# Casting v of batch 1 on GpSimd, asking for the second quarter of w_in between two casts, and one up step moved ahead of a down step

## The chip, the cores and the metric

The kernel runs on one core of a Trainium2 chip. Its engines work beside each other, each on its own queue and in the order of that queue: TensorE (matmuls and transposes into PSUM), VectorE and ScalarE (elementwise work, both may read PSUM), GpSimd (elementwise work on SBUF, and here the issue of the weights' DMAs), and SyncE (issues the other DMAs). The metric is the device time of one execution in microseconds (us); lower is better. An engine waits for another through semaphores.

## The reference

Two layers in a row. The first is causal attention with a sliding window of 128 and a linear bias per head, for 8 batches, 8 heads, 576 positions and 64 values per head. The second takes the 4608 tokens with their 8 x 64 = 512 attention outputs through a hidden layer of 2048:

```python
scores = scale * np.matmul(q, k.transpose(0, 1, 3, 2))
bias = slopes[:, None, None] * (-np.abs(rel).astype(np.float32))[None, :, :]
mask = (rel >= 0) & (rel < window)
scores = np.where(mask, scores + bias[None], -1000000000.0)
attn = softmax(scores)                       # written out in the reference
x = np.matmul(attn, v)                       # -> [B*S, H*D]
h = x @ w_in
g = h * np.clip(h + 3.0, 0.0, 6.0) / 6.0
out = g @ w_out
```

Inputs and output are float32 in DRAM.

## The kernel before

**Attention.** The unit of attention is a group g: two heads of one batch, four groups per batch, 32 in all. For each group the kernel computes transposed scores for the diagonal blocks (`scd`) and the blocks beside the diagonal (`sco`), exponentials on ScalarE (`pd`, `po`), and for some groups the mask by an affine select on GpSimd (L348 for `pd`, L358 for `po`). Groups 4 to 7 (batch 1) have their off-diagonal blocks masked through a table added on TensorE, so only their diagonal blocks are masked on GpSimd, by two selects per group. Then come the products with v, in which a column of ones beside v gives the sum of the exponentials; VectorE takes the reciprocal and scales (L406 and L407 in `attend`, L395 and L396 in `values`). `back` transposes the result into `xT`.

**v.** v of a batch comes by five DMAs (`load_tokens`, L112; 128 tokens each, the last 64) as float32 into one of four load buffers, and is cast to bf16 into `vbuf`. For batch 1 VectorE does this in five casts (`cast_v`, L177): pieces 0 to 3 after the off-diagonal exponentials of group 6, two ahead of each of two units of the hidden layer, and the last piece after that. For batches 2 to 7 GpSimd does it in three casts (`cast_tokens`, L183 twice and L186): two of 128 x 1024 values and one of 64 x 512.

**q and k** of batches 1 to 3 are loaded in double pieces (`load_double`, L98), cast on GpSimd (`prepare_double`, L223; for each of k and q two casts of 128 x 576), transposed on TensorE (`wide_double`, L248, or `double`, L236) and copied to `kTb` and `qTb`.

**Hidden layer.** The tokens are cut in nine tiles of 512. A tile has 16 ups and 16 downs. An up (`moe_up`) is four matmuls (L445) into `hps`, a ScalarE instruction (L464) and a VectorE product (L465) that writes one of 16 slices of `gbuf`. Up number ms needs columns ms x 128 of w_in, so ups 4 to 7 need its second quarter, 8 to 11 its third. A down (`moe_down`) is four matmuls (L477) and needs one of four quarters of w_out; four downs make a block of 128 output rows, after which the block is copied out (L492). The order of ups of one tile and downs of the tile before it is written out in `ORDER`, one string for each block; `fill(n)` takes the next n units from that list, at places written out in the attention code, so the order of all work on each engine is fixed.

**Weights.** w_in and w_out come in quarters by DMAs that GpSimd issues (L166, L171), with a cast to bf16 on the way. The first quarter of w_in is asked for among the casts of v of batch 0, the second after the four casts of the first double piece of batch 1 (`prepare_double(1, 0, ...)`), the third and fourth after the next four casts. The four quarters of w_out are asked for at the end of the loop over groups 4 to 6, after the casts of v. The buffer of w_out serves before that as the room for the exponentials of batch 0: slices 4 and 5 hold `pd` of group 1.

**Around it.** After the w_out issues GpSimd masks group 7, casts the double pieces of batch 2, and between them does a memset (L624) into a load buffer; v of batch 2 (SyncE) waits for that memset. The masks, casts and weight issues all stand in GpSimd's one queue in the order of the program.

Of the kernel before, what the change touches and what calls it, by code (L numbers as in the profile page):

```python
# [18 lines left out]
def kernel(  # L19
# [9 lines left out]
    nc = tc.nc  # L29
# [6 lines left out]
    NP = H // 2  # L36
# [18 lines left out]
    w_out_sb = perm.tile([128, n_ms, d_model], BF16)  # L55
# [94 lines left out]
    def warm_up(n):  # L150
        w = ps_av.tile([128, 128], FP32, tag="av", name="w")
        for _ in range(n):
            nc.tensor.matmul(w, lhsT=ident, rhs=ident, start=True, stop=True)
# [11 lines left out]
    def load_w_in(g):  # L165
        nc.gpsimd.dma_start(  # L166
            out=w_in_sb[:, :, ts(g, 512)],
            in_=moe_w_in[:, ts(g, 512)].rearrange("(k p) f -> p k f", p=128))

    def load_w_out(g):  # L170
        nc.gpsimd.dma_start(  # L171
            out=w_out_sb[:, ts(g, 4), :],
            in_=moe_w_out[ds(g * 512, 512), :].rearrange("(m p) d -> p m d", p=128))

    def cast_v(b, j, copy):
        n = min(128, S - j * 128)
        copy(out=vbuf[b % 2][:n, j, :, 0:D], in_=ld[b, "v"][:n, j, :, :])  # L177

    def cast_tokens(b, nm):
        s = ld[b, nm]  # L180
        if nm == "v":
            for lo in (0, 2):
                nc.gpsimd.tensor_copy(  # L183
                    out=vbuf[b % 2][:, lo:lo + 2, :, 0:D].rearrange("p j h d -> p (j h) d"),
                    in_=s[:, lo:lo + 2, :, :].rearrange("p j h d -> p (j h) d"))
            nc.gpsimd.tensor_copy(out=vbuf[b % 2][:LAST, 4, :, 0:D], in_=s[:LAST, 4, :, :])  # L186
            return
        for j in range(NQ):
            m = min(128, S - j * 128)
            nc.gpsimd.tensor_copy(out=tbuf[:m, :, j, :],  # L190
                                  in_=s[:m, j, :, :].rearrange("p (i e) d -> p i (e d)", e=2))
# [8 lines left out]
    def prepare(g, copies):  # L200
        for nm, copy in zip("qk", copies):
            pr = prs.tile([128, RT * D], BF16, tag=f"pr{nm}", name="pr",
                          padded_shape=[128, 2 * RT * D])
            copy(out=pr, in_=runs[nm][:, g % NP, :])
            st[g, nm] = pr
# [10 lines left out]
            copy(out=dst[:, hp, :, :].rearrange("p j c -> p (j c)")[:, 0:S].rearrange(  # L216
                "p (a t) -> p a t", t=RT), in_=tp.rearrange("p t a -> p a t"))

    def prepare_double(b, dp, copies, nms="kq"):
        for nm, copy in zip(nms, copies):  # L220
            pr = prs.tile([128, RT, 2 * D], BF16, tag=f"pr{nm}", name="pr2")
            for e in range(2):
                copy(out=pr[:, :, ts(e, D)],  # L223
                     in_=ldbuf["qk".index(nm)][:, ds((2 * dp + e) * RT * D, RT * D)].rearrange(
                         "p (t d) -> p t d", t=RT))
            st[b, dp, nm] = pr

    BANKS = {"h": ps_h, "av": ps_av, "o": ps_o}
# [31 lines left out]
    def tables_diag(g):  # L260
        scd = ps_sc.tile([128, 2, 512], FP32, tag="sc", name="scd")
        st[g, "scd"] = scd
        for e in range(2 if diag_tabled(g) else 0):
            t = tab[:, 2 * (g % NP) + e, 1:2, :]
            nc.tensor.matmul(scd[:, e, :].rearrange("p (j c) -> p j c", j=4), lhsT=ident,
                             rhs=t.to_broadcast([128, 4, 128]), start=True, stop=False)
# [26 lines left out]
    def tables_off(g):  # L293
        hp = g % NP
        sco = ps_sc.tile([128, 2, 512], FP32, tag="sc", name="sco")
        st[g, "sco"] = sco
        if full(g):
            for e in range(2):
                h = 2 * hp + e
                t = tab[:, h, 0:1, :]  # L300
                nc.tensor.matmul(sco[:, e, 128:512].rearrange("p (j c) -> p j c", j=3),
                                 lhsT=ident, rhs=t.to_broadcast([128, 3, 128]),
                                 start=True, stop=False)
                nc.tensor.matmul(sco[:, e, 0:128].rearrange("p (s c) -> p s c", s=2),
                                 lhsT=ident, rhs=tab[:, h, :, 0:64], start=False, stop=False)
# [26 lines left out]
    def exp_full(g):  # L332
        for e in range(2):
            exp_diag(g, e)
        exp_off_full(g)
# [113 lines left out]
    def up_begin(nt, ms, n):  # L449
        hps = ps_h.tile([128, NT], FP32, tag="h", name="hps")  # L450
        up_mms(nt, ms, 0, n, hps)
        begun[nt, ms] = hps, n
# [15 lines left out]
    def moe_down(nt, step):  # L468
# [10 lines left out]
        if part == 3:  # L479
# [11 lines left out]
            else:  # L491
                nc.vector.tensor_copy(out=osb, in_=ops[nt, sub])  # L492
                nc.sync.dma_start(out=out[rows, :], in_=osb)

    ORDER = [("UUDUDUDUD", "UUDUDUDUD", "UUDUDUDD", "UUDDDD"),
             ("DDDD", "UUDUDUDUD", "UUDUDUDUD", "UUDUDUDDUU"),
             ("DDDD",) * 4]
    units = [(0, moe_up, step) for step in range(16)]
    for nt in range(1, n_nt + 1):
        ups, downs = iter(range(16)), iter(range(16))  # L500
        for c in "".join(ORDER[0 if nt == 1 else 2 if nt == n_nt else 1]):
            units.append((nt, moe_up, next(ups)) if c == "U" else (nt, moe_down, next(downs)))
    at = [0]

    def fill(n):
        for _ in range(n):
            if at[0] == len(units):
                return
            nt, fn, step = units[at[0]]
            if fn is moe_up and done[0] < NP * (min((nt * NT + NT - 1) // S, B - 1) + 1):  # L510
                return
            fn(nt if fn is moe_up else nt - 1, step)
            at[0] += 1

    V, P, A = nc.vector.tensor_copy, nc.gpsimd.tensor_copy, nc.scalar.copy
# [24 lines left out]
    def first_batch():  # L540
        prepare(0, (V, A))
        warm_up(20)
        tables_diag(0)
        tables_off(0)
        warm_up(10)
        transposes(0, (V, A))
        scores_diag(0)
        prepare(1, (P, V))
        transposes(1, (V, V))
        scores_off(0)  # L550
        exp_full(0)
        scores_diag(1)
        prepare(2, (P, P))
        tables_off(1)
        transposes(2, (V, V))
        scores_off(1)
        exp_full(1)
        scores_diag(2)
        prepare(3, (P, V))
        tables_off(2)  # L560
        transposes(3, (V, V))
        scores_off(2)
        exp_full(2)
        scores_diag(3)
        scores_off(3)
        exp_full(3)
        cast_v(0, 0, V)
        cast_v(0, 1, P)
        load_w_in(0)
        cast_v(0, 2, V)  # L570
        cast_v(0, 3, V)
        cast_v(0, 4, P)
        for dp in range(2):
            for nm in "kq":
                load_double(1, dp, nm, nc.sync)
        load_tokens(1, "v")
        attend(0)
        attend(1)
        back(0)
        attend(2)  # L580
        back(1)
        prepare_double(1, 0, (P, P))
        load_w_in(1)
        attend(3)
        back(2)
        up_begin(0, 0, 3)
        back(3)
        wide_double(1, 0, "q", V)
        prepare_double(1, 1, (P, P))
        load_w_in(2)  # L590
        load_w_in(3)
        for dp in range(2):
            for nm in "kq":
                load_double(2, dp, nm, nc.sync)
        up_begin(0, 1, 3)
        done[0] = NP
        fill(1)
        wide_double(1, 0, "k", A)
        fill(2)

    def second_batch():
        for g in range(NP, 2 * NP - 1):
            if g < NP + 2:
                wide_double(1, 1, "kq"[g - NP], V)
            scores_diag(g)
            exp_diag(g, 0)
            exp_diag(g, 1)
            fill(1 if g == NP + 2 else 2)
            scores_off(g)
            exp_off_full(g)  # L610
            for n in range(2 if g == NP + 2 else 1):
                if g == NP + 2:
                    cast_v(1, 2 * n, V)
                    cast_v(1, 2 * n + 1, V)
                fill(1)
        cast_v(1, 4, V)
        for i in range(4):
            load_w_out(i)
        g = 2 * NP - 1
        scores(g)  # L620
        exp_diag(g, 0)
        exp_diag(g, 1)
        prepare_double(2, 0, (P, P))
        nc.gpsimd.memset(ldbuf[2][:, 0:1], 0.0)  # L624
        load_tokens(2, "v")
        prepare_double(2, 1, (P, P))
        for dp in range(2):
            load_double(3, dp, "k", nc.sync)
        load_tokens(3, "q")
        exp_off_full(g)  # L630
        fill(1)
        attend(NP)
        fill(1)
        attend(NP + 1)
        fill(1)
        back(NP)
        attend(NP + 2)
        fill(1)
        back(NP + 1)
        double(2, 0, "k", 0, "av", A)  # L640
        attend(NP + 3)
        back(NP + 2)
        double(2, 0, "k", 1, "av", A)
        wide_double(2, 0, "q", A)
        up_begin(1, 0, 3)
        back(2 * NP - 1)
        up_begin(1, 1, 3)
        done[0] = 2 * NP
        fill(2)
        scores_diag(2 * NP)  # L650
        scores_off(2 * NP)
# [98 lines left out]
```

## Time and profile before

| what | value |
|---|---|
| median of 3 runs | 335.48 us (335.27 to 336.54) |
| the profiled execution | 337.09 us, its span from first to last instruction 335.4 us |
| mean granted TensorE clock | 0.984 of full speed |
| TensorE matmuls busy | 314.2 us, 94% of the span |
| VectorE busy | 181.1 us, 54% |
| ScalarE busy | 198.5 us, 59% |
| GpSimd busy | 139.4 us, 42% |
| read from and written to DRAM | 36.70 MB and 9.44 MB |

Times in a timeline count from the start of the span. A row of it gives the start, the time until the end, the engine (PE is TensorE, DVE VectorE, ACT ScalarE, POOL GpSimd, SPq and POOLq the queues of SyncE and GpSimd), the line, the operation, what it writes and reads, and how many were merged; in brackets stands how long the engine was idle ahead of it, and what ended that. Shares are means over all stages: in the first 60 us the engines take turns at being late, and afterwards TensorE is busy nearly all of the time. The profile's busy time of a matmul is modelled, and neighbours overlap.

### The profile page before, as it was taken

Reading aid. Unit: us, or ns where it says so; the run is one execution under the profiler, and the core shown is the slowest. Engines: PE = TensorE matmul, PEld = TensorE weight load, DVE = VectorE, ACT = ScalarE, POOL = GpSimd, SP = SyncE. Lnnn points to the kernel's source line nnn. Section 1 sums busy time; section 2 is a strip of 40 time slices with the busy share of each in tenths; the row PEclk is TensorE's granted clock in tenths of the full one; section 3 lists DMA queues with packets and bytes.
Section 4 is the critical chain, followed back from the end, with each engine's and each line's share of the span. In section 5 each row is a group of like instructions: output and inputs, shape, how many; then the busy total and the mean of one; then the engine's idle time right before and its main releaser. Section 6 shows DMA issues by size and latency. Waiting matters only on the chain.

```text
span 335.4 us, 7019 instructions
## 1 busy us (share of the span) xinstructions
PE 314.2 (94%) x2707; PEld 169.2 (50%) x2747; DVE 181.1 (54%) x343; ACT 198.5 (59%) x339; POOL 139.4 (42%) x245
## 2 busy tenths in 40 slices
PE   7887938999999999999999999999999999999995
PEld 5463525544555455554577764454554444444442
DVE  6665597446434655466455554655556555445510
ACT  4746843677776775776577757675766344344401
POOL 8364390076459727573756375645333000000000
PEclk9998987999999999999999999999999999999999
DMA  7999999931999899989999997861021201000112
GB/s 286 203 336 223 323 159 221 245 99 50 211 199 221 182 201 226 227 160 220 222 164 171 209 226 162 172 153 53 33 71 44 71 29 37 31 31 33 62 53 73
DMA packets 128065, 51.08 MB, mean 152 GB/s; under 512 B 115616, under 2 KB 119968, under 8 KB 128032
## 3 DMA queue, kind: packets, MB, share of 16 engines
q1 hardware_dynamic: 122800, 44.61, 60.4%
q0 software_dynamic: 4224, 4.19, 8.0%
q10 hardware_dynamic: 1008, 1.84, 1.5%
q8 instruction: 21, 0.34, 0.5%
q14 instruction: 12, 0.10, 0.1%
HBM read 36.70 MB, written 9.44 MB: 138 GB/s over the span
## 4 chain that ended last, share of the span: by engine, by line
PE 80%; ACT 5%; DMA 4%; DVE 4%; POOL 3%; issue 2%; SPq 0%; POOLq 0%; DVEq 0%
PE ops L477 35%; PE hps L445 34%; PE scd L290 2%; DMA ldbuf<-in_q_dram 2%; DMA w_in_sb<-in_moe_w_in_dram 2%; PE av L385 2%; DVE vbuf L177 2%; PE av L377 2%; PE sco L322 2%; ACT r L464 1%; ACT xT L432 1%; DVE gbuf L465 1%; PE tb L426 1%; ACT kTb L238 1%; POOL pr L223 1%
## 5 line engine op out<-in xcount | busy, mean ns | idle before, releaser
L465 DVE SCALAR_TENSOR_TENSOR gbuf<-r,hps 128x512 bf16<-128x512 f32 x144 | 98.7, 686 | 108.2 <-ACT r L464 107.8
L464 ACT ACTIVATE r<-hps,bias 128x512 f32<-128x512 f32 x144 | 99.1, 690 | 91.3 <-PE hps L445 90.9
L445 PE MATMUL hps<-xT,w_in_sb 128*128 128x512 bf16 (+1 forms) x618 | 147.0, 362 | 4.9 <-DMA w_in_sb<-in_moe_w_in_dram 2.3
L477 PE MATMUL ops<-w_out_sb,gbuf 128*128 128x512 bf16 x558 | 139.2, 379 | 1.6 <-issue 1.1
L445 PEld LDWEIGHTS <-w_in_sb 128*128 128x128 bf16 x640 | 59.4, 99 | 57.8 <-issue 3.4
L477 PEld LDWEIGHTS <-gbuf 128*128 128x128 bf16 x576 | 53.6, 98 | 57.9
L348 POOL TENSOR_SCALAR_AFFINE_SELECT pd<-pd 128x512 bf16<-128x512 bf16 x48 | 30.1, 636 | 70.2 <-ACT pd L345 70.2
L358 POOL TENSOR_SCALAR_AFFINE_SELECT po<-po 128x512 bf16<-128x512 bf16 x48 | 30.5, 636 | 27.6 <-ACT po L355 26.8
L345 ACT ACTIVATE pd<-scd,bias_d 128x512 bf16<-128x512 f32 x48 | 32.1, 687 | 2.6 <-POOL vbuf L183 2.6
L355 ACT ACTIVATE po<-sco,bias_o 128x512 bf16<-128x512 f32 x48 | 33.3, 694 | 0.0
L492 DVE COPY osb<-ops 128x512 f32<-128x512 f32 x33 | 22.7, 688 | 18.7 <-PE ops L477 18.1
L190 POOL CAST tbuf<-ldbuf 128x512 bf16<-128x512 f32 (+1 forms) x45 | 25.5, 614 | 1.6 <-DMA qTb<-tbuf 1.6
L396 DVE TENSOR_TENSOR avs<-av,rc 128x384 bf16<-128x384 f32 (+1 forms) x48 | 23.5, 490 | 1.6
L385 PEld LDWEIGHTS <-pd 128*128 128x128 bf16 x192 | 14.3, 97 | 8.2 <-issue 0.5
L432 ACT COPY xT<-tb 128x576 bf16<-128x576 bf16 x13 | 8.3, 639 | 16.7 <-PE tb L426 16.7
L377 PE MATMUL av<-vbuf,po 128*128 128x65 bf16 x192 | 18.0, 193 | 0.0
L385 PE MATMUL av<-vbuf,pd 128*128 128x65 bf16 x192 | 17.3, 194 | 0.3 <-ACT kTb L238 0.2
L377 PEld LDWEIGHTS <-po 128*128 128x128 bf16 x192 | 14.3, 98 | 3.0 <-DVE avs L396 0.5
L361 ACT ACTIVATE p4buf<-sco,bias_d 128x64 bf16<-128x64 f32 x48 | 15.8, 329 | 0.0
L290 PEld LDWEIGHTS <-kTb 64*128 64x128 bf16 x256 | 7.2, 94 | 14.5 <-issue 10.8
L290 PE MATMUL scd<-qTb,kTb 64*128 64x128 bf16 x256 | 12.7, 219 | 1.8 <-DVE kTb L216 1.1
L223 POOL CAST pr<-ldbuf 128x576 bf16<-128x576 f32 x20 | 12.7, 664 | 3.9 <-DMA ldbuf<-in_k_dram 3.6
(93 smaller groups left out, 231.4 us busy)
## 6 DMA issues: line engine op xcount, KB each, us to landing
out_dram<-osb SPq DMA_DIRECT2D x33, 256.0 KB, 2.2
ldbuf<-in_v_dram SPq DMA_DIRECT2D x32, 256.0 KB, 5.3
ldbuf<-in_q_dram SPq DMA_DIRECT2D x20, 256.0 KB, 4.7
ldbuf<-in_k_dram SPq DMA_DIRECT2D x16, 256.0 KB, 4.7
ldbuf<-in_q_dram SPq DMA_DIRECT2D x12, 288.0 KB, 7.2
ldbuf<-in_k_dram SPq DMA_DIRECT2D x12, 288.0 KB, 7.6
w_in_sb<-in_moe_w_in_dram POOLq DMA_DIRECT2D x4, 512.0 KB, 8.3
w_out_sb<-in_moe_w_out_dram POOLq DMA_DIRECT2D x4, 512.0 KB, 9.2
```

The costliest lines, as they stand in the source:

```text
L190: nc.gpsimd.tensor_copy(out=tbuf[:m, :, j, :], in_=s[:m, j, :, :].rearrange("p (i e) d -> p i (e d)", e=2))
L290: nc.tensor.matmul(scd[:, e, ts(j, 128)], lhsT=kT[r, j, :], rhs=qT[r, j, :], start=first, stop=first or j == 3)
L345: nc.scalar.activation(out=pd[:, e, :, :].rearrange("p j c -> p (j c)"), in_=sc[:, e, :], func=ACT.Exp, bias=bias_d[:, h:h + 1], scale=scale)
L348: nc.gpsimd.affine_select(out=pd[:, e, :, :], in_=pd[:, e, :, :], pattern=[[0, 4], [1, 128]], channel_multiplier=-1, base=0, compare_op=AL ...
L355: nc.scalar.activation(out=po[:, e, :, :].rearrange("p j c -> p (j c)"), in_=sc[:, e, :], func=ACT.Exp, bias=bias_o[:, h:h + 1], scale=scale)
L358: nc.gpsimd.affine_select(out=po[:, e, :, :], in_=po[:, e, :, :], pattern=[[0, 4], [-1, 128]], channel_multiplier=1, base=-1, compare_op=A ...
L377: nc.tensor.matmul(out_av, lhsT=po[:, e, qt % 4, :], rhs=vb[:, qt - 1, h, :], start=True, stop=False)
L385: nc.tensor.matmul(out_av, lhsT=d, rhs=vb[:, qt, h, :], start=(qt == 0), stop=True)
L445: nc.tensor.matmul(hps[:, lo:hi], lhsT=w_in_sb[:, ks, ts(ms, 128)], rhs=xT[:, ks, ds(src, hi - lo)], start=(ks == 0), stop=(ks == n_ks - 1))
L464: nc.scalar.activation(out=r6, in_=hps, func=ACT.Relu, bias=bias3[:, 0:1], scale=1.0 / 6.0)
L465: nc.vector.scalar_tensor_tensor(out=gts[nt][:, ms, :], in0=r6, scalar=1.0, in1=hps, op0=ALU.min, op1=ALU.mult)
L477: nc.tensor.matmul(ops[nt, sub], lhsT=gts[nt][:, ms, ts(sub, 128)], rhs=w_out_sb[:, ms, :], start=(ms == 0), stop=(ms == n_ms - 1))
```

## The change

Three edits. First, v of batch 1 is cast by GpSimd in three casts (`cast_tokens(1, "v")`) after the two units that follow group 5's exponentials, in place of VectorE's five casts after those of group 6; the number of units that `fill` takes in each round stays. Second, the second quarter of w_in is asked for after the first of the four casts of `prepare_double(1, 0, ...)`; a one-column memset into slice 4 of the w_out buffer is put ahead of it. Third, in the order of tile 1's ups and tile 0's downs the first block has six ups in place of five, the additional one ahead of the last but one down, and the third block has three in place of four.

```diff
+    def second_w_in():
+        nc.gpsimd.memset(w_out_sb[:, 4, 0:1], 0.0)
+        load_w_in(1)
+
...
-    def prepare_double(b, dp, copies, nms="kq"):
+    def prepare_double(b, dp, copies, nms="kq", early=None):
         for nm, copy in zip(nms, copies):
             pr = prs.tile([128, RT, 2 * D], BF16, tag=f"pr{nm}", name="pr2")
             for e in range(2):
                 copy(out=pr[:, :, ts(e, D)],
                      in_=ldbuf["qk".index(nm)][:, ds((2 * dp + e) * RT * D, RT * D)].rearrange(
                          "p (t d) -> p t d", t=RT))
+                if early and (nm, e) == (nms[0], 0):
+                    early()
             st[b, dp, nm] = pr
...
-    ORDER = [("UUDUDUDUD", "UUDUDUDUD", "UUDUDUDD", "UUDDDD"),
+    ORDER = [("UUDUDUUDUD", "UUDUDUDUD", "UDUDUDD", "UUDDDD"),
...
-        prepare_double(1, 0, (P, P))
-        load_w_in(1)
+        prepare_double(1, 0, (P, P), early=second_w_in)
...
             scores_off(g)
             exp_off_full(g)
-            for n in range(2 if g == NP + 2 else 1):
-                if g == NP + 2:
-                    cast_v(1, 2 * n, V)
-                    cast_v(1, 2 * n + 1, V)
-                fill(1)
-        cast_v(1, 4, V)
+            fill(2 if g == NP + 2 else 1)
+            if g == NP + 1:
+                cast_tokens(1, "v")
         for i in range(4):
             load_w_out(i)
```

## The prediction

> **What bounds the kernel now.** I read the page first, then the time by stretches, then who waited for whom on TensorE, then each engine's timeline around the two waits found. The page's span, and stretches of the first 55 us (busy time of TensorE, its weight loads, VectorE, ScalarE and GpSimd, granted clock, DMA share, GB/s):
>
> ```profile
> span 335.4 us, 7019 instructions
> ```
> ```profile
> 30.00:35.00 5.00, 4.97 (x39) 2.76 (x39) 1.06 (x2) 2.40 (x3) 0.00 (x0) 0.66 1.24 205
> ...
> 40.00:45.00 5.00, 4.95 (x60) 2.62 (x59) 3.83 (x9) 5.00 (x9) 4.89 (x7) 1.00 0.88 198
> 45.00:50.00 5.00, 0.26 (x9) 0.17 (x6) 5.00 (x1) 1.01 (x2) 5.00 (x10) 0.84 1.14 182
> 50.00:55.00 5.00, 4.00 (x28) 2.16 (x28) 3.67 (x7) 0.69 (x1) 0.67 (x2) 0.50 1.22 200
> ```
>
> From some 60 us on the page's slices show TensorE at nine tenths or more, so whatever reaches TensorE earlier by then should reach the end earlier. Before that there are holes: from 45 to 50 there are 0.26 us of matmuls, and behind that the clock is 0.50; from 30 to 35 it is 0.66. TensorE's own waits, longest in total first, name what ended the two largest:
>
> ```profile
> PE wide L385 <- DVE vbuf L177: 5.7, 1, 5.7
> PE hps L445 <- DMA w_in_sb<-in_moe_w_in_dram: 2.3, 1, 2.3
> ```
>
> The first is the attention of group 4, waiting for the last cast of v. The group of v casts (shortest, median, longest in ns, first and last start), then GpSimd's timeline from that last start on:
>
> ```profile
> L177 DVE CAST vbuf<-ldbuf x8: 409/428/6218, 15.1 to 44.7; 128x512 bf16<-128x512 f32 x7, 64x512 bf16<-64x512 f32 x1
> ```
> ```profile
> 43.62 0.90 POOL L171 DMA_DIRECT2D w_out_sb<-in_moe_w_out_dram  x1
> 44.53 1.23 POOL L348 TENSOR_SCALAR_AFFINE_SELECT gbuf<-gbuf 128x512 bf16<-128x512 bf16 x2
> 45.70 2.49 POOL L223 CAST pr<-ldbuf 128x576 bf16<-128x576 f32 x4
> 48.14 0.09 POOL L624 MEMSET ldbuf<- 128x1 f32 x1
> 48.18 2.49 POOL L223 CAST pr<-ldbuf 128x576 bf16<-128x576 f32 x4
> ```
>
> A v cast takes 0.43 us at the median; the last, of half the size, takes 6.22. It starts at 44.7 while GpSimd works and ends at 50.9, just after GpSimd's unbroken row (44.53 to 50.67). I read it as shut out by GpSimd until that engine paused. TensorE's 5.7 us all come from this one instruction.
>
> The Trainium skill (SBUF — State Buffer, Who interferes with whom) says that a VectorE cast in a two-port mode and a GpSimd instruction exclude each other, and that the later one blocks until the first finishes. Taken literally the block would end with the first mask, at about 45.1; the trace has ten further GpSimd instructions pass first. Either a queue of them keeps the port, or the cast waited for something else: the second is rival E.
>
> **Part 1: v cast by GpSimd.** Five casts leave VectorE; three come to GpSimd, between the masks of groups 5 and 6. The same three for batch 2, with what follows, and a VectorE instruction beside them:
>
> ```profile
> 71.22 2.02 POOL L183 CAST vbuf<-ldbuf 128x1024 bf16<-128x1024 f32 x2
> 73.19 0.61 POOL L186 CAST vbuf<-ldbuf 64x512 bf16<-64x512 f32 x1
> 73.75 1.27 POOL L223 CAST pr<-ldbuf 128x576 bf16<-128x576 f32 x2
> ```
> ```profile
> 72.37 0.69 DVE L465 SCALAR_TENSOR_TENSOR gbuf<-r,hps 128x512 bf16<-128x512 f32 x1 [0.32 <-ACT r L464]
> ```
>
> Price on GpSimd: 2.02 + 0.61 = 2.6 us. The hole that takes it, ahead of group 6's masks; then the queues and the DMA issues between 27 and 28 us (KB each, us to landing):
>
> ```profile
> 40.10 1.23 POOL L348 TENSOR_SCALAR_AFFINE_SELECT gbuf<-gbuf 128x512 bf16<-128x512 bf16 x2 [2.92 <-ACT gbuf L345]
> ```
> ```profile
> q0 software_dynamic: 177, 0.17, 104.2%
> q1 hardware_dynamic: 149, 0.04, 17.5%
> issues: line engine op xcount, KB each, median us to landing
> w_in_sb<-in_moe_w_in_dram POOLq DMA_DIRECT2D x1, 512.0 KB, 11.1
> ldbuf<-in_v_dram SPq DMA_DIRECT2D x1, 128.0 KB, 12.1
> ```
>
> GpSimd is idle for 2.9 us, from 37.2 to 40.1, and 2.6 fit. But the last piece of v (128 KB) was issued before 27 and takes 12.1: it lands by 39, its cast ends by some 39.5. That is a **new wait** in GpSimd's queue. Behind it stand the masks of group 6, the four w_out issues, the masks of group 7, the casts of batch 2, and the memset that lets SyncE ask for v of batch 2. As part 2 brings TensorE and ScalarE earlier, group 6's masks will wait for the cast, no longer for their exponentials, and everything behind comes forward by only 0.6 us.
>
> What is late next? VectorE. Its next product needs the first row's result, and each attention group needs the pair of the second fence; the last of four such pairs is the third row:
>
> ```profile
> 45.30 0.71 ACT L464 ACTIVATE r<-hps,bias 128x512 f32<-128x512 f32 x1
> ```
> ```profile
> 51.47 0.20 DVE L406 RECIPROCAL rcw<-wide 128x10 f32<-128x10 f32 x1
> 51.70 0.82 DVE L407 TENSOR_TENSOR avs<-wide,rcw 128x640 bf16<-128x640 f32 x1
> ```
> ```profile
> 58.87 0.82 DVE L407 TENSOR_TENSOR avs<-wide,rcw 128x640 bf16<-128x640 f32 x1
> ```
>
> A pair takes 1.05 from 51.47 to 52.52, a product about 0.6 (0.69 less the overlap of neighbours); four of each make 6.6 us. Begun at 46.0 they end at 52.6; now they end at 59.7. **Gain 7.1 us.** The ends: 5.7 if the wait alone goes; 7.7 if the slow clock goes as well (4.00 us busy at 0.50, half of them lost) and TensorE alone sets the pace. I take 7.1, by VectorE's rows, the engine that is full there.
>
> The Trainium skill (Perfetto Trace Analysis, Optimizing Scalar/DVE Operations) warns that shifting work between these two engines may not help, since they share a port. The row at 72.37 speaks against it here: 0.69 us, the usual 686 ns of its group, while GpSimd casts v. The case is rival D.
>
> **Part 2: the second quarter of w_in asked for earlier.** GpSimd's order, the quarter's transfer in the chain that ended last, TensorE's next transposes, and the DMA rate at that time:
>
> ```profile
> 17.22 0.67 POOL L223 CAST pr<-ldbuf 128x576 bf16<-128x576 f32 x1 [0.88 <-DMA ldbuf<-in_k_dram]
> 20.60 2.11 POOL L223 CAST pr<-ldbuf 128x576 bf16<-128x576 f32 x3 [2.72 <-DMA ldbuf<-in_k_dram]
> ```
> ```profile
> 22.65 7.33 DMA w_in_sb<-in_moe_w_in_dram
> ```
> ```profile
> 22.77 0.68 PE L248 MATMUL tp<-ident,pr 128*128 128x128 bf16 x9
> ```
> ```profile
> 20.00:21.00 1.00, 0.83 (x23) 0.80 (x21) 0.91 (x2) 0.64 (x1) 0.40 (x1) 1.00 1.04 408
> ```
>
> The memset (the one at 48.14 took 0.09) waits for group 1's attention matmuls, which TensorE's timeline ends near 18.4. GpSimd idles for 2.72 us just there, so memset and issue (at most 0.90, as for w_out) cost its queue nothing. The transfer starts near 18.4 in place of 22.65 and lands between 25.7 (7.3, as now) and 29.5 (11.1, the slowest row above): TensorE no longer waits for it. Removed: 2.3 us, and the clock of 0.66 behind it (4.97 us with a third lost, 1.7), together 4.0. More it cannot be, for ScalarE is full from 40 to 45 (5.00 of 5).
>
> What it moves: the quarter is 1 MB as read, 0.5 as written, and now goes among the pieces of k and q while the engines carry 408 GB/s. It can take 0 to 2.6 us from them. The q cast ends at 22.7 and its transposes start at 22.77, so all of that reaches TensorE. I take the middle, 1.3. The third quarter's issue stands behind later q casts and slides the same way; for a wait there I take 0.4 (0 to 0.8). **Gain 4.0 - 1.3 - 0.4 = 2.3 us**, ends 0.6 and 4.0, and 0 if q is held for as long as w_in was.
>
> **Part 3: one up step earlier.** The same matmuls in another order. Two ups now follow each other within the first block; the later needs the PSUM bank that this copy frees, and the block's last down, which comes one step later, needs w_out's last quarter (issues from 44.0 to 44.4 us):
>
> ```profile
> 65.96 0.72 DVE L238 COPY kTb<-tp 128x512 bf16<-128x512 bf16 x1
> ```
> ```profile
> 68.65 1.03 PE L477 MATMUL ops<-w_out_sb,gbuf 128*128 128x512 bf16 x4
> ```
> ```profile
> w_out_sb<-in_moe_w_out_dram POOLq DMA_DIRECT2D x1, 512.0 KB, 12.9
> ```
>
> The copy ends at 66.7, and the up would begin at about 66.9. The quarter, issued at 43.62, lands at 56.5; the down, 9.4 earlier, would come at 59.3 even in its old place. So 0, ends plus and minus 1.0, one such group's length.
>
> **Sum:** 7.1 + 2.3 + 0 = 9.4 us. The profiled execution took 337.09, its span 335.4 (1.7 around it): 326.0 of span, 327.7 with the rest. The median of the runs is 335.48, 1.6 under the profiled one, so the forecast is **326.1**. What could cap it is k of batch 3 (issues from 59.0 to 59.5 us):
>
> ```profile
> ldbuf<-in_k_dram SPq DMA_DIRECT2D x1, 288.0 KB, 5.7
> ```
>
> Issued before 59, it lands by 64.7, or 64.1 with the memset 0.6 earlier; its cast at 73.75 wants it at 64.35. Gains beyond some 9.6 are partly given back there.
>
> **Rivals.** (B) Asking for w_in earlier only exchanges waits, q being held for as long as TensorE waited: part 1 alone, 328.4. For it: from 27 to 28 w_in's queue had 104% of the time against 17.5% for v's. Against: q's pieces are not v's. (C) q is hardly held and TensorE sets the pace: 7.7 + 4.0, less half of what is beyond 9.6, makes 10.7: 324.8. (D) The change does not do what it says, because a full GpSimd queue shuts out any VectorE instruction: the product due at 46.0 stands until 50.7 in the cast's place and all is as before, 335.5. Against: the row at 72.37. (E) The 6.22 us were a wait for v itself, landing at 50.3. Then its cast holds GpSimd until 50.9, and the megabyte put ahead makes that up to 53.5. Masks, w_out issues, masks and two casts (1.2 + 3.6 + 1.2 + 1.3) end at 60.8. TensorE wants those casts here:
>
> ```profile
> 57.37 0.44 PE L236 MATMUL tp<-ident,pr 128*128 128x128 bf16 x5
> ```
>
> That is 3.4 late: 338.9, slower; it turns slower once v lands after 49.5. Against: the landing by 39. The skill's literal lock rule leaves room for E; the cast's end beside the end of GpSimd's row does not.
>
> **Chances.** Forecast 0.50 (324.9 to 327.5), B 0.25, C 0.18, D 0.04, E 0.03. The range 323.7 to 329.5 takes in the forecast, B and C with the ends of part 3, and leaves out D and E. Faster by over 0.5% (1.7 us, about what a measurement of this kernel can tell from no change) 0.93, the same 0.04, slower 0.03.
>
> **What would show it.** Right: no VectorE instruction above 1.4 us and no wait of TensorE for vbuf; GpSimd's last v cast ending near 39.5; no clock of 0.5 at 50 us; the wait for w_in gone, with a shorter one for the q cast near 23; the transposes of 57.37 near 48. Wrong: a wait for w_in as long as before, or for its third quarter (B); a product of 5 us beside GpSimd's casts (D); GpSimd idle ahead of v's cast until past 49 (E); TensorE waiting for w_out, v of batch 2 or k of batch 3, where part of the gain would end.

## The result, and the profile after

Median 326.53 us (325.98 to 326.96, 4 runs) against 335.38 for the kernel before (334.7 to 336.54, 4 runs of it). The ratio is 0.9732, with a 95% interval of 0.9701 to 0.9763: 9.0 us faster, between 8.0 and 10.0. The forecast was 326.1.

The page's head after the change, and the stretches that had the holes:

```profile
span 324.2 us, 7015 instructions
## 1 busy us (share of the span) xinstructions
PE 311.6 (96%) x2707; PEld 168.5 (52%) x2747; DVE 173.9 (54%) x338; ACT 198.0 (61%) x339; POOL 141.2 (44%) x249
```
```profile
30.00:35.00 5.00, 4.84 (x55) 2.82 (x56) 4.30 (x7) 4.76 (x8) 2.13 (x4) 1.00 1.22 198
...
45.00:50.00 5.00, 4.50 (x74) 3.54 (x74) 4.36 (x9) 4.23 (x8) 4.22 (x8) 1.00 1.19 190
50.00:55.00 5.00, 5.00 (x48) 2.66 (x47) 2.05 (x4) 3.02 (x5) 0.00 (x0) 1.00 1.22 203
```

From 45 to 50 us TensorE is busy for 4.50 of 5 us where it had 0.26, and the granted clock is 1.00 in all three. TensorE's two longest waits are now small ones from the start and from the downs:

```profile
PE w L153 <- POOL ident masks.py:199: 1.4, 1, 1.4
PE ops L483 <- issue: 1.1, 7, 0.2
```

GpSimd's timeline around the new casts (L187 and L190 are the casts of v, L354 the masks, L171 the issues for w_out, L227 the casts of batch 2, L626 the memset that releases v of batch 2):

```profile
34.12 1.04 POOL L187 CAST vbuf<-ldbuf 128x1024 bf16<-128x1024 f32 x1
37.40 1.04 POOL L187 CAST vbuf<-ldbuf 128x1024 bf16<-128x1024 f32 x1 [2.24 <-DMA ldbuf<-in_v_dram]
38.38 0.61 POOL L190 CAST vbuf<-ldbuf 64x512 bf16<-64x512 f32 x1
38.95 1.21 POOL L354 TENSOR_SCALAR_AFFINE_SELECT gbuf<-gbuf 128x512 bf16<-128x512 bf16 x2
40.12 2.99 POOL L171 DMA_DIRECT2D w_out_sb<-in_moe_w_out_dram  x4
43.08 1.26 POOL L354 TENSOR_SCALAR_AFFINE_SELECT gbuf<-gbuf 128x512 bf16<-128x512 bf16 x2
44.26 2.50 POOL L227 CAST pr<-ldbuf 128x576 bf16<-128x576 f32 x4
46.69 0.11 POOL L626 MEMSET ldbuf<- 128x1 f32 x1
46.73 2.48 POOL L227 CAST pr<-ldbuf 128x576 bf16<-128x576 f32 x4
```

The wait in GpSimd's queue is there: 2.24 us for v to land. The last v cast ends at 38.99. Group 6's masks follow with no pause, so they wait for the cast and no longer for ScalarE. Counted with the w_out issues, GpSimd's unbroken row runs from 37.40 to 49.21. The part behind the issues, which held VectorE's cast in the kernel before (44.53 to 50.67), is as long as it was, 6.1 us from 43.08 to 49.21, and it now hurts nobody. The issues themselves held no cast: in the kernel before, four of VectorE's v casts ran beside them (41.27 to 44.52) in 0.41 to 0.57 us each. VectorE's fourth attention pair ends at 49.45 in place of 59.69, although it works beside that row:

```profile
48.63 0.82 DVE L413 TENSOR_TENSOR avs<-wide,rcw 128x640 bf16<-128x640 f32 x1
```

The second quarter of w_in, on GpSimd (L176 is the new memset), then its DMA row (KB, us to landing), then the transposes of q that the forecast expected to be held up:

```profile
19.06 0.10 POOL L176 MEMSET w_out_sb<- 128x1 bf16 x1 [1.50 <-PE wide L391]
19.10 0.74 POOL L166 DMA_DIRECT2D w_in_sb<-in_moe_w_in_dram  x1
20.80 2.02 POOL L227 CAST pr<-ldbuf 128x576 bf16<-128x576 f32 x3 [0.95 <-DMA ldbuf<-in_k_dram]
```
```profile
w_in_sb<-in_moe_w_in_dram POOLq DMA_DIRECT2D x1, 512.0 KB, 9.1
```
```profile
23.79 0.67 PE L254 MATMUL tp<-ident,pr 128*128 128x128 bf16 x9
```

Issued at 19.10, the quarter lands at 28.2. It takes 9.1 us in place of 7.3 but starts 3.6 earlier. In this execution TensorE waits no longer for it. The q cast ends at 22.82, as before the change (22.71), and the transposes start without a wait. They start a microsecond later than before because attention in this execution began as much later, ahead of anything that was changed: its first product with v comes at 17.89, against 16.77 in the profile of before. Executions differ by that much here; a second profile of the kernel before (before_again, below) has 17.77.

### The profile page after: what moved, and what is told of

Its sections match the earlier page's. It is cut to its first block, busy times and chain, and to the rows that moved or that the text cites. A ratio compares the mean times of both kernels' runs of the same rounds, so it can differ in the third digit from the quotient of the medians.

```text
span 324.2 us, 7015 instructions
## 1 busy us (share of the span) xinstructions
PE 311.6 (96%) x2707; PEld 168.5 (52%) x2747; DVE 173.9 (54%) x338; ACT 198.0 (61%) x339; POOL 141.2 (44%) x249
## 4 chain that ended last, share of the span: by engine, by line
PE 88%; ACT 5%; DVE 4%; issue 2%; POOL 0%; POOLq 0%
PE ops L483 38%; PE hps L451 36%; PE scd L296 3%; PE av L391 2%; ACT xT L438 2%; PE av L383 2%; PE sco L328 2%; ACT r L470 2%; PE tb L432 1%; PE w L153 1%; ACT kTb L244 1%; DVE qTb L220 1%; PE sco L307 1%; DVE kTb L220 1%; PE tp L254 1%
## 5 line engine op out<-in xcount | busy, mean ns | idle before, releaser
L451 PE MATMUL hps<-xT,w_in_sb 128*128 128x512 bf16 (+1 forms) x619 | 144.1, 357 | 2.3 <-ACT xT L438 0.6
L354 POOL TENSOR_SCALAR_AFFINE_SELECT pd<-pd 128x512 bf16<-128x512 bf16 x48 | 30.0, 633 | 61.1 <-ACT pd L351 61.1
L187 POOL CAST vbuf<-ldbuf 128x1024 bf16<-128x1024 f32 x14 | 14.2, 1040 | 2.2 <-DMA ldbuf<-in_v_dram 2.2
```

Of the source, the lines that this page charges most:

```text
L354: nc.gpsimd.affine_select(out=pd[:, e, :, :], in_=pd[:, e, :, :], pattern=[[0, 4], [1, 128]], channel_multiplier=-1, base=0, compare_op=AL ...
L451: nc.tensor.matmul(hps[:, lo:hi], lhsT=w_in_sb[:, ks, ts(ms, 128)], rhs=xT[:, ks, ds(src, hi - lo)], start=(ks == 0), stop=(ks == n_ks - 1))
```

## The experiments

Ten runs beside the two kernels. The medians of the kernel before lay between 335.8 and 336.1 us in these sessions, so gains are read from ratios; 0.01 of ratio is 3.36 us.

| run | median us | ratio to before, 95% interval |
|---|---|---|
| p1_only | 328.37 | 0.9769 (0.9736 to 0.9801) |
| p2_only | 334.39 | 0.9941 (0.9915 to 0.9967) |
| p3_only | 334.95 | 0.9971 (0.995 to 0.9993) |
| p1_p2 | 326.67 | 0.9718 (0.9687 to 0.975) |
| v4_act | 329.56 | 0.9812 (0.9763 to 0.9861) |
| pause | 329.56 | 0.9811 (0.9768 to 0.9854) |
| long_row | 338.21 | 1.008 (1.0053 to 1.0106) |
| v_dve_early | 327.5 | 0.9762 (0.9715 to 0.981) |
| w_in_ahead | 326.9 | 0.9728 (0.9691 to 0.9765) |

The tenth, before_again, is a single execution of the kernel before, 336.21 us.

### The three parts alone

**p1_only** has the edit of `second_batch` alone:

```diff
-                    cast_v(1, 2 * n, V)
-                    cast_v(1, 2 * n + 1, V)
...
-        cast_v(1, 4, V)
+            if g == NP + 1:
+                cast_tokens(1, "v")
```

> Only v of batch 1 moves to GpSimd; w_in and the order as before. My theory (the 6.2 us cast was shut out by GpSimd's unbroken row): no wait of TensorE for vbuf, no VectorE instruction above 1.4 us, the wait for w_in of about 2.3 us stays with its slow clock; 7.1 us faster than before, about 328.3. Rival (the cast waited for v itself): GpSimd sits ahead of its last v cast until about 50, and the time is 335 or more.

It was 7.7 us faster (0.9769; 6.7 to 8.9). The only wait for vbuf left, 0.2 us, is for v of batch 0. The longest wait is where the second quarter of w_in is first used, 1.5 us; the profile puts it down to a copy that had ended, but the weight load ahead of the same matmul waited 2.0 us for w_in's DMA, so the DMA is the likelier releaser. Its waits, and the stretch behind that wait:

```profile
PE hps L445 <- DVE kTb L250: 1.5, 1, 1.5
```
```profile
30.00:35.00 5.00, 5.00 (x46) 2.68 (x47) 2.76 (x4) 3.75 (x6) 0.65 (x2) 1.00 1.23 202
```

The clock behind that wait is 1.00, not slow. That part of the expectation was wrong, and it comes back in before_again.

**p2_only** has the edits of `prepare_double` and `first_batch` alone:

```diff
-        prepare_double(1, 0, (P, P))
-        load_w_in(1)
+        prepare_double(1, 0, (P, P), early=second_w_in)
```

> Only the second quarter of w_in is asked for earlier. My theory: the wait for w_in goes, and the long v cast on VectorE stays at about 6 us but begins and ends some 3 us earlier, since GpSimd's row moves with ScalarE; 2.3 us faster, about 333.1 (ends 331.4 and 335.4). Rival B (the wait is only exchanged for one on q's cast): TensorE waits 1 us or more near 23 us and the time is 335.4. Third: the stall on v swallows the gain, because GpSimd's row ends at the same time as before.

2.0 us faster (0.9941; 1.1 to 2.9). VectorE's long cast, the end of GpSimd's row, and GpSimd's casts of k and q near 20 us:

```profile
41.50 6.23 DVE L181 CAST vbuf<-ldbuf 64x512 bf16<-64x512 f32 x1
```
```profile
44.96 2.49 POOL L227 CAST pr<-ldbuf 128x576 bf16<-128x576 f32 x4
```
```profile
20.50 2.17 POOL L227 CAST pr<-ldbuf 128x576 bf16<-128x576 f32 x3 [0.94 <-DMA ldbuf<-in_k_dram]
```

The cast still takes 6.2 us, and GpSimd's row has moved with it: row's end 47.45, cast's end 47.73. It starts 3.2 us earlier than in the profile of before, but 1.8 earlier than in before_again (43.34), which did not have the slow clock at 30 us; that is the fairer comparison for a gain of 2.0. So the stall did not swallow the gain. The casts end at 22.67 as before, so q is not held: the wait for w_in was not exchanged for another.

**p1_p2** has both of these and the old order; **p3_only** has only the new order:

```diff
-    ORDER = [("UUDUDUDUD", "UUDUDUDUD", "UUDUDUDD", "UUDDDD"),
+    ORDER = [("UUDUDUUDUD", "UUDUDUDUD", "UDUDUDD", "UUDDDD"),
```

> Both moves, the order of ups and downs as before. My theory: the same as with all three, 326.5 within 0.5. Rival: the order is needed once the first downs come 10 us earlier, because the last quarter of w_out lands at about 55.5; then a wait for w_out of 0.5 to 1.5 us shows and the time is 327 to 328.

> Only the order of ups and downs. My theory: no difference, 335.4 within 1. Rival: the two ups in a row wait for a PSUM bank, and it is slower by up to 1 us.

The time of p1_p2 is not told apart from that of all three (326.67 and 326.53 us; 0.9718 and 0.9732 of before, each in its own session), and no wait for w_out shows. For p3_only the median is 1.0 us under before (0.2 to 1.7 by the interval), which alone is little to go on. The traces say more, if the span is counted from the start of the first down, which leaves out everything ahead of the new order:

| run | first down starts | span | from there to the end, before rounding |
|---|---|---|---|
| old order: before | 62.66 | 335.4 | 272.7 |
| before_again | 61.77 | 334.5 | 272.7 |
| p1_only | 53.43 | 326.1 | 272.7 |
| p2_only | 60.19 | 332.9 | 272.7 |
| p1_p2 | 52.15 | 324.9 | 272.7 |
| new order: after | 52.03 | 324.2 | 272.2 |
| p3_only | 60.73 | 332.9 | 272.2 |
| v_dve_early | 52.84 | 325.1 | 272.2 |
| w_in_ahead | 52.16 | 324.4 | 272.2 |

The other old-order profiles, v4_act, pause and long_row, give 272.7 too. The new order is worth **0.5 us**, in every profile. It comes in two steps: from the first down to group 10's scores p1_p2 takes 9.75 us and after 9.54; from there to group 11's 8.02 and 7.75. In the first stretch a run of eight matmuls of ups shows a small hold, which after's row of eight does not have; p1_p2's row, then after's:

```profile
59.00 2.10 PE L451 MATMUL hps<-xT,w_in_sb 128*128 128x512 bf16 x8
```
```profile
59.74 1.89 PE L451 MATMUL hps<-xT,w_in_sb 128*128 128x512 bf16 x8
```

In p1_p2 the second of these two ups starts at 60.08, just after a VectorE product has ended at 60.02; in the second stretch an up starts at 65.27, just after one has ended at 65.21. So both holds look like ups waiting for VectorE to free their PSUM bank; no run tests that alone.

### What held VectorE's cast

Three kernels leave the casts where they were in the kernel before and change one thing each. **v4_act** gives the last piece to an engine that GpSimd could not hold, if GpSimd was the cause:

```diff
-        cast_v(1, 4, V)
+        cast_v(1, 4, A)
```

> The kernel before, with only the last piece of v of batch 1 (64 x 512) cast by ScalarE at its old place in the program; the other four stay on VectorE. My theory: what held the cast was GpSimd, which does not hold ScalarE: the cast takes about 0.7 us and ends by 46.5, TensorE's wait for vbuf falls from 5.7 to under 1.5 us, and the time is 6 to 7.5 us under before, 328 to 329.5. Rival (v itself late): ScalarE sits idle before that cast until about 50, and the time stays at 335.

ScalarE's row for that cast:

```profile
41.51 0.61 ACT L177 CAST vbuf<-ldbuf 64x512 bf16<-64x512 f32 x1
```

It ends at 42.12, with no pause ahead of it, so v was there some 8 us before VectorE's cast had ended in the kernel before (50.95, and 49.55 in before_again). The kernel is 6.3 us faster than before (0.9812; 4.7 to 8.0), at the low edge of what was expected. v itself was not late.

**long_row** makes GpSimd's row longer by casting four pieces of batch 2 a second time:

```diff
         prepare_double(2, 1, (P, P))
+        for nm in "kq":
+            for e in range(2):
+                P(out=st[2, 1, nm][:, :, ts(e, D)],
+                  in_=ldbuf["qk".index(nm)][:, ds((2 + e) * RT * D, RT * D)].rearrange(
+                      "p (t d) -> p t d", t=RT))
```

> The kernel before, with four casts of batch 2 done twice on GpSimd (the same values written again), so that its unbroken row is 2.5 us longer. My theory (VectorE's cast waits until the row ends): the cast takes 8.7 us in place of 6.2, ending with the row, TensorE waits 8.2 us for it, and the time is 2.5 us over before, about 338. By the rule that the later one waits only for the instruction that holds the port, or if v itself is late: the cast stays at 6.2 us and the time at 335.4.

VectorE's cast, and GpSimd's added casts:

```profile
43.30 8.65 DVE L177 CAST vbuf<-ldbuf 64x512 bf16<-64x512 f32 x1
```
```profile
49.18 2.49 POOL L629 CAST pr<-ldbuf 128x576 bf16<-128x576 f32 x4
```

The row ends at 51.67, the cast at 51.95; TensorE waits 8.2 us for it, and the kernel is 2.7 us slower than before (1.8 to 3.6). An instruction of some 0.4 us of work was held by fifteen instructions of another engine, one after the other.

**pause** keeps all the casts and gives GpSimd one reason to stand still:

```diff
+        P(out=warm[:LAST, :], in_=vbuf[1][:LAST, 4, 0, 0:1])
         prepare_double(2, 0, (P, P))
         nc.gpsimd.memset(ldbuf[2][:, 0:1], 0.0)
```

> The kernel before, with one more GpSimd instruction ahead of the casts of batch 2: it copies one column of the last piece of v from vbuf, so GpSimd pauses once until VectorE's last v cast is done; all casts stay where they were. My theory (that cast needs a pause in GpSimd's queue, nothing else): it takes under 2 us in place of 6.2, ending within 0.5 us of the end of group 7's masks; TensorE's wait for vbuf falls from 5.7 to under 1.5 us, and the time to 328 to 330. Rival (v late, or the cast slow by itself): the cast still takes 6 us, GpSimd stands still until then with its casts behind it, and the time is 336 or more.

VectorE's cast, and GpSimd around it:

```profile
43.50 1.31 DVE L177 CAST vbuf<-ldbuf 64x512 bf16<-64x512 f32 x1
```
```profile
43.29 1.23 POOL L348 TENSOR_SCALAR_AFFINE_SELECT gbuf<-gbuf 128x512 bf16<-128x512 bf16 x2
44.87 0.18 POOL L623 CAST warm<-vbuf 64x1 f32<-64x1 bf16 x1 [0.35 <-DVE vbuf L177]
45.33 2.50 POOL L223 CAST pr<-ldbuf 128x576 bf16<-128x576 f32 x4 [0.28 <-POOL warm L623]
```

The masks end at 44.52, the cast at 44.81. A pause of 0.35 us on one engine takes 4.9 us off an instruction of another, and 6.4 us off the kernel (0.9811; 4.9 to 7.8).

In before, p2_only, long_row and pause alike the cast ends 0.28 or 0.29 us after GpSimd's unbroken work does. What held it here was the row of GpSimd instructions without a gap, not one of them, not the data, and not the cast itself.

### Could VectorE have kept the casts?

**v_dve_early** is the changed kernel with VectorE's five casts at GpSimd's new place:

```diff
-                cast_tokens(1, "v")
+                for j in range(NQ):
+                    cast_v(1, j, V)
```

> All three edits, but v of batch 1 is cast by VectorE in five casts at the same place in the program (after the two units behind group 5's exponentials) in place of GpSimd's three. My theory: GpSimd has a hole there, so a cast takes 0.4 to 0.7 us; but VectorE stands in its order until the last piece of v has landed at about 38.5, with the products for groups 5 and 6 behind it, up to 4 us late; they hold the PSUM banks of the ups, so TensorE waits 1 to 3 us: 327.5 to 329.5. Rival: VectorE has the room (busy 2.1 of 5 us from 35 to 40), and it is as fast as after, 326.5, or a little faster since GpSimd's masks and w_out issues come earlier.

327.5 us is 1.0 over after, and the intervals of the two overlap, so by the times it is not told apart; it lies at the low edge of what was expected. In the profiles its first down comes 0.8 us later than after's. The five casts, and group 6's two masks beside them:

```profile
36.95 2.83 DVE L181 CAST vbuf<-ldbuf 128x512 bf16<-128x512 f32 x5
```
```profile
36.95 1.68 POOL L354 TENSOR_SCALAR_AFFINE_SELECT gbuf<-gbuf 128x512 bf16<-128x512 bf16 x2 [2.92 <-ACT gbuf L351]
```

Five casts take 2.83 us instead of about 2.1, and two masks 1.68 instead of 1.22: each engine held the other a little. They took turns. The second cast, and the two masks one by one:

```profile
37.28 0.86 DVE L181 CAST vbuf<-ldbuf 128x512 bf16<-128x512 f32 x1
```
```profile
36.95 0.91 POOL L354 TENSOR_SCALAR_AFFINE_SELECT gbuf<-gbuf 128x512 bf16<-128x512 bf16 x1 [2.92 <-ACT gbuf L351]
```
```profile
37.82 0.82 POOL L354 TENSOR_SCALAR_AFFINE_SELECT gbuf<-gbuf 128x512 bf16<-128x512 bf16 x1
```

The cast ends at 38.14, 0.28 us after the first mask (37.86), and the second mask, which follows the first without a gap, is the one held. So here VectorE got in between two GpSimd instructions. The same shows at 16 us in p1_only, where a VectorE cast of v of batch 0 ends at 16.77, 0.28 us after a GpSimd cast (16.48) that another follows without a gap. A row without gaps therefore does not always keep a VectorE cast out; why the one at 44.73 in the kernel before was not let in after the first mask is open.

So most of the gain comes from taking the cast out of GpSimd's unbroken row; which engine does it matters little.

### Does w_in hold q?

**w_in_ahead** asks for the second quarter earlier still, ahead of all four casts:

```diff
         cast_v(0, 4, P)
+        load_w_in(1)
...
-        prepare_double(1, 0, (P, P), early=second_w_in)
+        prepare_double(1, 0, (P, P))
```

> All three edits, but the second quarter of w_in is asked for ahead of all four casts of the first double piece, near 16.5 us in place of 19, without the memset. My theory, as the prediction had it (a quarter put among the pieces of q and k takes time from them): the q cast ends 1 to 2 us later than 22.8, TensorE waits as long ahead of its transposes, and the time is 1 to 2 us over after, 327.5 to 328.5. Rival (the quarter's packets take nothing from q's pieces, or the pieces have slack): no such wait, and 326.5.

GpSimd's timeline, and TensorE's transposes of q:

```profile
16.54 0.74 POOL L166 DMA_DIRECT2D w_in_sb<-in_moe_w_in_dram  x1
17.81 0.66 POOL L227 CAST pr<-ldbuf 128x576 bf16<-128x576 f32 x1 [0.52 <-DMA ldbuf<-in_k_dram]
20.44 1.44 POOL L227 CAST pr<-ldbuf 128x576 bf16<-128x576 f32 x2 [1.97 <-DMA ldbuf<-in_k_dram]
22.45 0.67 POOL L227 CAST pr<-ldbuf 128x576 bf16<-128x576 f32 x1 [0.57 <-DMA ldbuf<-in_q_dram]
```
```profile
23.17 0.68 PE L254 MATMUL tp<-ident,pr 128*128 128x128 bf16 x9 [0.43 <-POOL pr L227]
```

The wait ahead of the transposes is 0.43 us, not 1 to 2, and not clearly the quarter's: the q cast ends at 23.12, in before_again at 23.16, and long_row, which asks for w_in at the old time, has a wait of 0.55 there. What the quarter holds up are the pieces behind: of the eight pieces of k and q the last lands at 27.77, after the change at 26.14, and in the seven profiles with w_in at its old time at 25.1 to 25.9. TensorE also waits 0.8 us for the third quarter of w_in, which is issued at 28.44 in place of 26.80, behind the later q casts. The time is the same as after's. Asked for at 19, as in the change, the quarter delays nothing that shows in these first casts: they end at 22.82, against 22.71 before.

### The clock behind the shorter wait

**before_again** is the kernel before, unchanged.

> The kernel before, profiled once more: whether the granted clock of 0.66 from 30 to 35 us follows from the wait for w_in of 2.3 us. If it does: 0.6 to 0.7 again. If it is a matter of that one execution: 1.00 with about the same wait, and a span of 333 to 334 in place of 335.4. The stall of 5.7 us on the v cast and the clock of about 0.5 behind it come again in both.

The two waits, and the stretches behind each:

```profile
PE wide L385 <- DVE vbuf L177: 5.7, 1, 5.7
PE hps L445 <- DMA w_in_sb<-in_moe_w_in_dram: 1.6, 1, 1.6
```
```profile
30.00:35.00 5.00, 4.84 (x45) 2.63 (x46) 2.68 (x5) 3.52 (x6) 0.43 (x1) 1.00 1.24 205
...
50.00:55.00 5.00, 5.00 (x38) 2.93 (x37) 2.74 (x6) 1.32 (x3) 0.00 (x0) 0.51 1.22 209
```

The slow clock behind the 5.7 us comes again. The one behind the wait for w_in does not: 1.00. Seven profiled executions here have that wait, between 1.5 and 2.3 us long (before, before_again, p1_only, p3_only, v4_act, pause, long_row); only the first has a slow clock from 30 to 35. So the wait does not bring it each time.

Nor does it belong to that one execution alone. Every run's mean clock is on record. Of 32 later executions of the kernel before, 7 have the 0.984 of that first profile and take 336.5 to 337.4 us; the other 25 have 0.988 to 0.994 and a median of 335.7, 1.5 us less, about what the slow stretch would cost. Executions whose clock is lower by 0.004 to 0.005, and that take 1 to 2 us more than their neighbours, also occur in other kernels that still wait for w_in (p1_only 1 of 4, p3_only 1 of 9, v4_act 2 of 4, pause 2 of 4; the clocks of long_row vary too, without such a step in time). Among the 24 executions of the kernels that ask for w_in earlier there is none. Where in these executions the clock was lower is not on record, but it fits a slow clock that follows the wait in some executions and not in others.

## Why the prediction was right

**Part 1, forecast 7.1, measured 7.7.** The cause, that the cast stood until GpSimd's row ended, holds in three kernels that change nothing else: another engine for the cast, a longer row, one pause. Why it was not let in between two instructions of that row, as casts were in v_dve_early, stays open. The new wait for v in GpSimd's queue was forecast, and is there (2.24 us); everything behind it came forward by 1.2 us (w_out issues 41.27 to 40.12), the forecast having 0.6. The size is near the forecast's upper end, TensorE's sum, and not VectorE's: 5.7 for the wait and about 2.0 for the half clock behind it. pause agrees: it takes 4.9 us off the wait, the slow clock goes with it, and the gain is 6.4.

**Part 2, forecast 2.3, measured 2.0, by two errors that met.** The price of q, 1.3 us, was too large by all of it: the first q pieces were not held, and even w_in_ahead shows a wait of only 0.43. What the quarter took, it took from later pieces of k and q, for which TensorE does not wait yet. They made the third quarter's issue slide, as forecast, from 26.09 (26.40 in before_again) to 26.80, but the 0.4 for a wait there did not come. Against that stood 1.7 us for a slow clock that the profile of before shows, but which six of seven profiles, and 25 of 32 later executions of that kernel, do not have. What is left is the wait itself, 1.5 to 2.3 us, and not quite all of it: a wait for the second quarter of 0.5 us stays in the profile of p1_p2, and 0.2 in that of v_dve_early. That the two errors met is luck. A single profile cannot tell which of its rows belong to the kernel and which to the execution.

**Part 3, forecast 0, measured 0.5.** I looked only for new waits and took the old order as free of any; it had two holds, of 0.2 and 0.3 us. That lay within the ends of plus and minus 1.0.

**The sum, forecast 9.4, measured 9.0 (8.0 to 10.0).** The parts alone add to 7.7 + 2.0 + 0.5 = 10.2, and p1_p2's ratio gives 9.5, so they add up within what these intervals can tell. In the traces nothing after 60 us gave back what came earlier: from the first down on all old-order profiles take 272.7 us, whether that down starts at 52 or at 63. The possible cap, k of batch 3, did not act.

**The rivals.** B (waits exchanged) falls by p2_only. D (a full queue holds any VectorE instruction) falls by the profile after: four products and four attention pairs run at their usual lengths beside a row of 6.1 us, as long as the one that held the cast. E (v late) falls by v4_act and pause. C's mechanism, q hardly held and TensorE setting the pace, is what happened; its time, 324.8, was too low, mainly because it counted a slow clock that most executions do not have.

## What to carry to other kernels

An instruction that takes ten times its group's median is worth a look before any engine's total: ask whose unbroken work ends just where it ends. Before a VectorE cast from SBUF to SBUF is put beside GpSimd, look for gaps in GpSimd's queue; if it has none, move the cast to another engine or place, or give GpSimd one short reason to wait. And before a slow stretch is counted as a cost of the kernel, take a second profile of the same kernel, and look at the clock of every run on record.

## What the runs showed of the hardware

A VectorE cast between SBUF tiles that is caught by GpSimd work can stand through a whole row of GpSimd instructions, until GpSimd's queue has a gap: it ended 0.28 to 0.29 us after that gap opened, whether it was held for 1.0 us (pause) or for 8.4 (long_row). It need not: in v_dve_early and p1_only a cast got in between two back-to-back GpSimd instructions, and ended 0.28 us after the first. The Trainium skill (SBUF — State Buffer, Who interferes with whom) has the later one block until the first finishes. The two places in v_dve_early and p1_only agree with that; the long casts differ, and there the measurement decides. In the profile after, VectorE's instructions that read PSUM run beside GpSimd's casts at their usual 0.69 and 0.82 us.

TensorE's granted clock fell behind each stall of 5.7 us or more (to between 0.50 and 0.73 from 50 to 55 us), but behind waits of 1.5 to 2.3 us in only one of seven profiles.
